# A decode kernel at the memory's pace: three attention pairs with P as the weight, one more unit held on the chip, and new schedule tables

## The chip, the cores and the metric

One core of one Trainium2 chip. The metric is device time in microseconds (us); lower is better. The kernel before was run three times: 304.89 us median, from 302.9 to 305.69.

## The reference

Two layers, each an attention block with a cached K and V and then a gated block, on 4 sequences of one new token each. The weights are the same in both layers, and so are K and V.

```python
B, Sq, D = 4, 1, 512;  Hq, Hkv, Sk, Dh = 32, 8, 4096, 128;  F = 1792
def attn(x):   # x: layer-normed
    q = (x @ wq) -> heads;  k, v repeated 4 times over the heads
    p = softmax(q k^T * Dh**-0.5);  o = p v
    return o @ wo
def glu(x):
    return (sigmoid(x @ w_gate) * (x @ w_up)) @ w_down
for _ in range(2):
    x = x + attn(layernorm(x))
    x = x + glu(layernorm(x))
```

For one sequence b and one K/V head u, K and V have 4096 x 128 bf16 values each, 1 MB. 4 x 8 heads make 32 MB of K and 32 MB of V, and both layers need all of them: 128 MB, if nothing is kept.

## The kernel before, in words

**Units and pairs.** A unit is one head of one sequence in one layer; a pair is two neighbouring heads of a sequence. There are 32 units and 16 pairs in a layer, so 64 units and 32 pairs (`NP`) in all; an entry of `ORDER` is (layer, sequence, pair of heads), and its place in the list is the pair's position. The pairs are worked off in the order of `ORDER`; layer 1 of a sequence may begin as soon as its own layer 0 and its own gated block are done, so layers and sequences are interleaved.

**Slots and held units.** K and V units are loaded whole into 12 slots of 1 MB of on-chip memory. Once the last q of the second layer is computed, the four slices of `wq` become four further slots (`wq_done`). `RET` names for each sequence the heads whose K or V stay in their slot from layer 0 to layer 1 and so are not loaded twice. `LOADS` is the order of all loads, written out by hand as a string: k, v, o (an eighth of `wo`) and s (a part of the three other weights). `pump()` issues loads from SyncE's queue (SP) for as long as a slot is free; each load waits for the last reader of its slot.

**One step.** Step k (the loop over `plan`) works on the scores and the softmax of pair k and, one step later, on PV of pair k-1; `EARLY` marks pairs whose PV is done in their own step. K is turned in place by VectorE's 32x32 transposes (`k_turn`, line 1164), the scores are 16 matmuls a unit (line 1180), the row maximum is a reduction and two small matmuls (1217 to 1253), the exponential runs on ScalarE (1265), P is turned by two matmuls (`ptrans`, 1310) and copied in 16 pieces by ScalarE and VectorE (1338, 1344). PV (`pv`, line 1414) takes **V as the weight**: per unit 32 weight loads of 128x128, and as the moving operand four columns of P, repeated up to the width that `PV_WIDE` gives (32, 48 or 64 columns; the result is in the first four). `normalise` (1505) multiplies by the inverse row sums, `wo_mm` applies `wo` either with `wo` as the weight (1566) or, where `WO_ROW` is set, as rows (1536, a copy at 1545 and a turn of four matmuls at 1549).

**Between the layers.** The gated block of a sequence and its q for layer 1 are 23 small pieces (`pass_steps`: layer norm, gate, up, down, q as rows). `PLACES` says for each piece in which step and at which of nine places (0 to 8) of the step it is issued; `do_steps(k, w)` issues what stands at a place. `FILL` adds matmuls of no use to a place: `fill(n)` multiplies the identity by itself n times (line 1199). `STEP` packs per step where K is turned and PV stands.

**A branch that is not taken.** For `PV_WIDE` below 2, `pv` already has the other form: P as the weight (8 or 16 columns a matmul) and 256 or 512 columns of V moving, into separate strips of 32 rows of a bank; and `o_turn` brings the rows back into columns: ScalarE copies the bank into the slot of the V just read, and 2 or 4 f32 matmuls with a selecting matrix `o_sel` write the columns. No pair of the kernel before uses it, so `o_sel` isn't built.

**The tail.** In step 32 the PV of the last pair (`pv_last`, line 1441) reads V in quarters, the last `wo` product is added up, and the gated block of all four sequences follows (920 to 2053). `LAST`, from the last entry of `STEP`, says whether the `wo` product that is still open goes before or after the first `pv_last`.

Of the kernel before, what the change touches and what calls it, by code (L numbers as in the profile page):

```python
# [5 lines left out]
dt = mybir.dt  # L6
# [13 lines left out]
]  # L20

ORDER = [
    (0, 0, (0,)),
    (0, 0, (3,)),
    (0, 0, (2,)),
    (0, 1, (1,)),
    (0, 0, (1,)),
    (0, 2, (0,)),
# [4 lines left out]
    (0, 1, (2,)),  # L33
    (1, 0, (3,)),
    (1, 0, (0,)),
    (0, 2, (2,)),
    (1, 1, (2,)),
    (1, 1, (3,)),
    (0, 2, (1,)),
    (0, 2, (3,)),  # L40
    (1, 1, (0,)),
    (1, 1, (1,)),
    (0, 3, (3,)),
    (1, 2, (3,)),
    (0, 3, (0,)),
    (0, 3, (2,)),
    (0, 3, (1,)),
    (1, 2, (1,)),
    (1, 2, (0,)),
    (1, 2, (2,)),  # L50
# [12 lines left out]
    ),  # L63
    (
# [10 lines left out]
    ),  # L75
    (
# [16 lines left out]
    "kooookokovkvkkvokokvvvkksvvkksvvksskkssk",  # L93
    "vvvkkvkvkkvvkkvkvkvkvvkvkvkvkvkvkvvkvvkk",
    "kkkvvvvkkvkvkvvkkvvkkvkkvvkvvkkkvvvkvkkv",
    "kvvvkkvkvvkkkvkkvvvvvv",
# [35 lines left out]
WO_ORDER = (1, 3, 7, 2, 4, 0, 6, 5)  # L132

WO_TURN = (
# [7 lines left out]
PV_WIDE = (  # L142
# [4 lines left out]
)  # L147
# [9 lines left out]
WSUM = (  # L157
    (7, 8), (28, 0), (22, 5), (18, 7),
    (22, 0), (29, 7), (27, 4), (29, 7),
# [3 lines left out]
AHEAD = ((29, 2), (30, 8), (32, 4))  # L163
# [147 lines left out]
def bass_interleave_layers__gqa_block_cached__glu_gated_glu__decode_kernel(  # L311
# [85 lines left out]
    norm = sbt([P, KD + 10, Bn], dt.float32, "norm")  # L397
    sq_sb, newt = norm[:, 0:KD + 1, :], norm[:, KD + 1:, :]
    lnsum, blk_f, vpe, nt_a, nt_b, nt_c, nt_y, rs = [newt[:, i, :] for i in range(8)]
    y0i = newt[:, 8, :].bitcast(dt.int32)  # L400
# [259 lines left out]
    def head_masks():  # L660
# [15 lines left out]
        for u in range(2):  # L676
# [30 lines left out]
        id4 = ident_bf.rearrange("p (u e w) -> p u e w", u=2, e=2)  # L707
        dve(
            lambda e: e.tensor_tensor(sel_f[:, :, :], id4[:, :, 0, 0:2], id4[:, :, 1, 0:2], ALU.add),
# [3 lines left out]
        if SEL:  # L713
            dve(
                lambda e: e.tensor_tensor(o_sel[:, :, :], id4[:, :, 0, 0:SEL], id4[:, :, 1, 0:SEL], ALU.add),
                reads=IDENT,
                writes=["o_sel"],
            )
# [754 lines left out]

    def o_turn(g):
        p = g % 2
        many = 2 - PV_WIDE[g]
        s = stage.pop()
        o_raw = slot[s].bitcast(dt.float32)[:, 0:2 * P * many]
        act(lambda e: e.activation(o_raw, O_ps[p][:, 0:2 * P * many], ACTF.Copy), reads=[f"O{p}"], writes=slot_keys(s))
# [16 lines left out]
    def normalise(g):  # L1496
        if PV_WIDE[g] < 2:
            o_turn(g)
# [633 lines left out]
```

## Time and profile before

| | |
|---|---|
| three runs | 302.9, 304.89, 305.69 us |
| profiled execution, span from first to last instruction | 306.1 us (no other time of it is known) |
| mean granted TensorE clock | 0.883 |
| busy | PE 73%, PE's weight loads 51%, VectorE 67%, ScalarE 43%, GpSimd 9% |
| read from memory | 116.66 MB, 381 GB/s over the span |

The profile's first part gives busy time by engine; the second cuts the span in 40 slices of 7.65 us, with the granted TensorE clock, the busy share of the DMA engines and the GB/s of each; the fourth follows the chain of work that ended last back from the end. A matmul's busy time is a model, since matmuls overlap; how long a row of matmuls takes is read from the timeline, where neighbours of one line are merged.

### The profile page before, as it was taken

How to read it: one execution, taken by the hardware profiler on the slowest of the kernel's cores; microseconds unless marked ns; L12 is line 12 of the kernel's file. 1: busy time of each engine (PE TensorE's matmuls, PEld its weight loads, DVE VectorE, ACT ScalarE, POOL GpSimd, SP SyncE). 2: the span in 40 equal slices, each digit the busy share in tenths (PEclk: the TensorE clock that was granted, in tenths of full speed). 3: DMA queues.
4: the chain of work that ended last, by engine and by line, in shares of the span. 5: the costliest groups of instructions: out<-in, count | busy, mean ns of one | idle time of the engine just before them, and what ended most of it. 6: DMA issues, size and time to landing. Idle time of an engine off the chain costs nothing.

```text
span 306.1 us, 11460 instructions
## 1 busy us (share of the span) xinstructions
PE 224.3 (73%) x4993; PEld 157.6 (51%) x4993; DVE 205.7 (67%) x600; ACT 131.2 (43%) x521; POOL 26.0 (9%) x107
## 2 busy tenths in 40 slices
PE   0384386864687888688886777888868688987886
PEld 0331043543464466566554554665546456556676
DVE  4755677885766368875854997566788668357743
ACT  1031243552205246564451874627772443646310
POOL 0000000000000010000001110001000000012200
PEclk9999999999579897979999857589788979599977
DMA  7999999999999979999999999999999999999900
GB/s 283 420 397 415 422 414 416 418 418 421 418 416 403 388 295 418 423 415 416 388 394 378 415 422 421 419 418 422 420 416 418 413 412 415 400 345 411 377 18 3
DMA packets 20094, 117.40 MB, mean 384 GB/s; under 512 B 1992, under 2 KB 1996, under 8 KB 7500
## 3 DMA queue, kind: packets, MB, share of 16 engines
q1 hardware_dynamic: 20044, 116.67, 93.9%
q8 instruction: 39, 0.64, 0.8%
q14 instruction: 11, 0.09, 0.1%
HBM read 116.66 MB, written 0.00 MB: 381 GB/s over the span
## 4 chain that ended last, share of the span: by engine, by line
DMA 45%; PE 30%; DVE 12%; SPq 5%; ACT 4%; issue 3%; POOL 0%; POOLq 0%; DVEq 0%; ACTq 0%
DMA slot<-in_A_v_cache_dram 22%; DMA slot<-in_A_k_cache_dram 12%; PE O_ps L1414 9%; DMA wd<-in_B_w_down_dram 6%; DVE slot L1164 6%; DMA wo<-in_A_wo_dram 5%; PE S_ps L1180 5%; ACT pT L1344 2%; SPq L550 2%; SPq L528 2%; PE M_ps L636 2%; PE O_ps L1566 2%; PE M_ps L1034 1%; PE M_ps L1087 1%; DVE wo L651 1%
## 5 line engine op out<-in xcount | busy, mean ns | idle before, releaser
L1164 DVE STREAM_TRANSPOSE slot<-slot 128x1024 f32<-128x1024 f32 (+1 forms) x61 | 100.9, 1663 | 7.0 <-DMA slot<-in_A_k_cache_dram 6.9
L1344 ACT ACTIVATE pT<-PT 32x64 bf16<-32x64 f32 x392 | 84.3, 215 | 31.9 <-PE PT L1310 26.9
L1414 PE MATMUL O_ps<-pT,slot 128*128 128x32 bf16 (+2 forms) x1888 | 65.8, 190 | 16.2 <-DMA slot<-in_A_v_cache_dram 9.6
L1414 PEld LDWEIGHTS O_ps<-pT,slot 128*128 128x128 bf16 x1888 | 59.6, 101 | 23.3 <-DMA slot<-in_A_v_cache_dram 10.6
L1180 PE MATMUL S_ps<-slot,qz 128*32 128x256 bf16 x1008 | 48.9, 329 | 12.5 <-DVE slot L1164 7.2
L1265 ACT ACTIVATE pe<-S_ps,small 128x256 bf16<-128x256 f32 x32 | 15.2, 474 | 63.3 <-DVE small L1253 63.2
L1180 PEld LDWEIGHTS S_ps<-slot,qz 128*32 128x32 bf16 x1008 | 25.3, 107 | 24.8 <-DVE slot L1164 9.2
L1279 POOL TENSOR_TENSOR small<-small 128x1 f32<-128x1 f32 x64 | 12.4, 193 | 217.6 <-ACT pe L1265 215.1
L646 ACT ACTIVATE wo<-M_ps 128x512 bf16<-128x512 f32 x14 | 8.3, 595 | 35.0 <-PE M_ps L636 35.0
L1338 DVE CAST pT<-PT 32x64 bf16<-32x64 f32 x88 | 19.4, 221 | 5.6 <-PE PT L1310 4.1
L1566 PE MATMUL O_ps<-oT,wo 128*128 128x32 bf16 x576 | 19.7, 188 | 1.1 <-issue 0.5
L636 PE MATMUL M_ps<-wo,row 64*128 64x512 bf16 x56 | 13.3, 565 | 9.1 <-DVE wo L651 5.5
L1566 PEld LDWEIGHTS O_ps<-oT,wo 128*128 128x128 bf16 x576 | 18.2, 101 | 2.1 <-DVE oT L1505 1.1
L1217 DVE TENSOR_REDUCE small<-S_ps 128x1 f32<-128x256 f32 x32 | 13.2, 413 | 8.0 <-PE S_ps L1180 7.8
L903 POOL TENSOR_TENSOR qz<-qc,norm 128x128 bf16<-128x128 bf16 x32 | 12.6, 399 | 45.5 <-ACT qc L889 45.5
L1240 PE MATMUL MS<-row_max,mask_f 128*128 128x16 bf16 x64 | 6.6, 176 | 13.1 <-DVE row_max L1223 12.6
L651 DVE CAST wo<-M_ps 128x512 bf16<-128x512 f32 x14 | 9.5, 680 | 9.6 <-PE M_ps L636 9.5
L1505 DVE TENSOR_TENSOR oT<-O_ps,rden 128x8 bf16<-128x8 f32 x31 | 4.9, 159 | 14.4 <-PE O_ps L1414 9.8
L1240 PEld LDWEIGHTS MS<-row_max,mask_f 128*128 128x128 bf16 x64 | 4.3, 107 | 19.2 <-DVE row_max L1223 17.7
L1199 PE MATMUL MS<-ident_bf 128*128 128x256 bf16 x69 | 12.2, 316 | 0.4
L1310 PE MATMUL PT<-ident_bf,pe 128*128 128x128 bf16 x64 | 10.0, 245 | 2.9 <-ACT pe L1265 2.6
L1253 DVE CUSTOM_DVE_ANT_0 row_max<-MS,small 128x16 bf16<-128x16 f32 x32 | 7.0, 217 | 7.3 <-PE MS L1240 7.1
(143 smaller groups left out, 231.1 us busy)
## 6 DMA issues: line engine op xcount, KB each, us to landing
slot<-in_A_v_cache_dram SPq DMA_DIRECT2D x49, 1024.0 KB, 12.5
slot<-in_A_k_cache_dram SPq DMA_DIRECT2D x43, 1024.0 KB, 11.3
wq<-in_A_wq_dram SPq DMA_DIRECT2D x4, 1024.0 KB, 7.8
wo<-in_A_wo_dram SPq DMA_DIRECT2D x8, 512.0 KB, 15.8
wq<-in_A_v_cache_dram SPq DMA_DIRECT2D x3, 1024.0 KB, 12.3
slot<-in_A_v_cache_dram SPq DMA_DIRECT2D x8, 256.0 KB, 13.6
wg<-in_B_w_gate_dram SPq DMA_DIRECT2D x2, 896.0 KB, 18.9
wu<-in_B_w_up_dram SPq DMA_DIRECT2D x2, 896.0 KB, 16.2
```

The source lines that it names most:

```text
L636: (lambda h, i, rows: lambda e: e.matmul(ps[h][:, :], lhsT=spread_w[i][rows, :], rhs=wo_sb[rows, c + i, :], start=(i == 0), stop=(i == 1), ...
L651: lambda e: e.tensor_copy(wo_sb[:, c + 1, :], ps[1][:, :]),
L903: lambda e: e.tensor_tensor(qz_sb[z][:, :, 0:4 * REP].rearrange("p i (a r) -> p i a r", r=REP), qc_sb[:, b, u:u + 2, :, :].rearrange("p u ...
L1164: dve(lambda e: e.transpose(kf, kf), writes=[f"s{st}"])
L1180: (lambda t, b2, e_, w0, s: lambda e: e.matmul(S_ps[p][32 * s:32 * s + 8 * REP, 0:2 * P], lhsT=qzf[:, w0:w0 + 8 * REP], rhs=ktv[:, :, s, : ...
L1217: lambda e: e.tensor_reduce(m, S_ps[p][:, 0:2 * P], AX.X, ALU.max),
L1265: lambda e: e.activation(to, frm, ACTF.Exp, bias=nm_sb[p], scale=exp_scale, accum_out=sm_sb[p][0],),
L1279: (lambda n: lambda e: e.tensor_tensor(sm_sb[p][n + 1], sm_sb[p][n], top(sm_sb[p][n]), ALU.subtract))(n),
L1338: (lambda dst, frm: lambda e: e.tensor_copy(dst, frm))(dst, frm),
L1344: (lambda dst, frm: lambda e: e.activation(dst, frm, ACTF.Copy))(dst, frm),
L1414: (lambda x, c, j: lambda e: e.matmul(O_ps[p][:, ul * OW:ul * OW + PV_WIDE[g]].rearrange("p (w n) -> p w n", n=REP), lhsT=vv[:, x * JG + c ...
L1566: (lambda c, r: lambda e: e.matmul(wide_out(O_ps[p], OWO + c, nb), lhsT=wo_sb[:, u * REP + r, bass.ds(2 * P * (c // 2) + c % 2, P, step=2) ...
```

## The change

It does five things.

1. `RET`: V of head 4 of sequence 3 is held as well (31 units in place of 30), so one load of 1 MB is gone.
2. `PV_WIDE`: the pairs at positions 1, 27 and 30 take P as the weight (1: 256 columns of V move in each matmul; 0: 512 columns).
3. `divide()` for such a pair is `o_copy` (ScalarE's copy) alone; the matmuls that turn the rows back and `normalise` come at one of four times that `TURN` gives for the step: 0 at once, 1 after `ptrans`, 2 after place 7, 3 in the next step ahead of `sums`.
4. `sel` becomes the first two columns of `o_sel` and two small vectors of the layer norm share a place, which frees the memory for `o_sel`.
5. All tables are chosen anew: the order of the pairs (a few neighbours change places), of the loads, the places of the 23 pieces, which pieces of P VectorE copies (`SHARE`), the fills (122 matmuls in 27 places; before 70 in 16), the form of `wo` by pair, `STEP`, and `LAST` (from 5 to 1: the open `wo` product goes after the first `pv_last`).

```diff
-    {"k": (0, 1, 2, 3, 4, 5), "v": (5,)},
+    {"k": (0, 1, 2, 3, 4, 5), "v": (4, 5)},
...
 PLACES = [
...
-        (1, 8), (2, 1), (2, 1), (2, 1), (2, 1), (2, 1),
-        (2, 2), (2, 2), (2, 2), (2, 3), (2, 4), (2, 6),
-        (2, 8), (3, 1), (3, 2), (3, 3), (3, 3), (3, 5),
-        (3, 5), (3, 5), (3, 5), (3, 6), (3, 6),
+        (1, 8), (2, 1), (2, 1), (2, 1), (2, 1), (2, 1), (2, 1), (2, 1), (2, 2),
+        (2, 4), (2, 4), (2, 6), (2, 6), (3, 0), (3, 0), (3, 0), (3, 0), (3, 0),
+        (3, 0), (3, 1), (3, 3), (3, 6), (3, 6),
...
 WO_ROW = (
...
-    2, 0, 0, 2, 1, 0, 0, 2,
-    0, 0, 0, 2, 0, 0, 1, 0,
-    0, 0, 0, 0, 1, 2, 0, 2,
+    2, 0, 0, 0, 0, 0, 1, 2,
+    0, 0, 2, 0, 0, 0, 0, 0,
+    0, 0, 0, 0, 2, 0, 1, 2,
...
 PV_WIDE = (
-    32, 48, 48, 48, 32, 48, 48, 32,
-    64, 48, 64, 64, 48, 48, 32, 32,
-    32, 48, 64, 32, 32, 64, 64, 48,
-    32, 32, 64, 48, 64, 48, 64, 48,
+    32, 1, 32, 32, 64, 48, 48, 32,
+    32, 64, 64, 64, 64, 48, 64, 48,
+    32, 32, 64, 48, 48, 48, 64, 48,
+    64, 48, 64, 0, 64, 64, 0, 32,
...
 FILL = {
-    (3, 8): 1, (4, 6): 6, (5, 1): 6, (5, 2): 5, (5, 8): 8, (6, 0): 4,
-    (6, 4): 6, (6, 7): 2, (8, 2): 8, (11, 1): 8, (11, 5): 1, (12, 1): 5,
-    (18, 7): 3, (22, 2): 4, (25, 5): 2, (33, 1): 1,
+    (0, 1): 4, (2, 8): 1, (3, 3): 1, (4, 0): 1, (5, 8): 9, (7, 4): 5,
+    (7, 8): 1, (8, 2): 10, (12, 1): 6, (13, 8): 4, (14, 1): 1, (14, 7): 8,
+    (16, 0): 7, (16, 7): 2, (16, 8): 10, (17, 1): 5, (21, 0): 2, (21, 7): 3,
+    (22, 0): 1, (22, 7): 11, (22, 8): 1, (24, 1): 1, (24, 7): 14, (26, 2): 11,
+    (29, 6): 1, (32, 8): 1, (33, 8): 1,
...
+TURN = (
+    3, 0, 2, 3, 0, 2, 3, 2,
+    3, 3, 1, 0, 1, 3, 0, 1,
+    1, 0, 1, 2, 0, 2, 0, 1,
+    0, 0, 3, 0, 1, 1, 2, 3,
+    3,
+)
...
-    sel_f = sbt([P, 2, 2], dt.float32, "sel")
-    SEL = 2 * REP * any(w < 2 for w in PV_WIDE)
-    o_sel = sbt([P, 2, SEL], dt.float32, "o_sel") if SEL else None
+    SEL = 2 * REP * (2 - min(PV_WIDE)) if min(PV_WIDE) < 2 else 0
+    o_sel = sbt([P, 2, max(SEL, 2)], dt.float32, "o_sel")
+    sel_f = o_sel[:, :, 0:2]
...
+    def o_copy(g, k):
+        p = g % 2
+        s = stage.pop()
+        o_raw = slot[s].bitcast(dt.float32)[:, 0:2 * P * (2 - PV_WIDE[g])]
+        act(
+            lambda e: e.activation(o_raw, O_ps[p][:, 0:2 * P * (2 - PV_WIDE[g])], ACTF.Copy),
+            reads=[f"O{p}"],
+            writes=slot_keys(s),
+        )
+        turning.append((g, s, o_raw, k))
+
+    def o_turn():
+        if not turning:
+            return
+        g, s, o_raw, k = turning.pop()
...
-        S.group("pe", fns, reads=slot_keys(s) + ["o_sel"], writes=[f"O{p}"])
+        S.group("pe", fns, reads=slot_keys(s) + ["sel"], writes=[f"O{p}"])
         free.append(s)
         pump()
+        normalise(g)
+        normed[seq[2 * g]] = k
...
         def divide():
+            if PV_WIDE[vg] < 2:
+                o_turn()
+                o_copy(vg, k)
+                if TURN[k] == 0:
+                    o_turn()
+                return
             normalise(vg)
             normed[seq[2 * vg]] = k
...
+        if TURN[k] == 1:
+            o_turn()
         wo_at(3)
         do_steps(k, 7)
         second_turn(2)
+        if TURN[k] == 2 or vg in ends:
+            o_turn()
```

The pieces of sequence 3's pass, the last of the four lists of `PLACES`, are shown since the prediction speaks of them; the step of (2, w) is step 26 and that of (3, w) is step 27 in both kernels.

More of the change, by code (lines that the diff above doesn't have):

```diff
@@ L33 @@
     (0, 1, (2,)),
+    (1, 0, (0,)),
     (1, 0, (3,)),
-    (1, 0, (0,)),
     (0, 2, (2,)),
+    (1, 1, (3,)),
     (1, 1, (2,)),
-    (1, 1, (3,)),
     (0, 2, (1,)),
     (0, 2, (3,)),
+    (1, 1, (1,)),
     (1, 1, (0,)),
-    (1, 1, (1,)),
     (0, 3, (3,)),
     (1, 2, (3,)),
+    (0, 3, (1,)),
     (0, 3, (0,)),
     (0, 3, (2,)),
-    (0, 3, (1,)),
     (1, 2, (1,)),
+    (1, 2, (2,)),
     (1, 2, (0,)),
-    (1, 2, (2,)),
     (1, 3, (2,)),
@@ L129 @@
 )
-WO_ORDER = (1, 3, 7, 2, 4, 0, 6, 5)
+WO_ORDER = (
+    4, 1, 0, 2, 3, 6, 7, 5,
+)
 WO_TURN = (
[4 rows of a table removed]
+    (1, 8), (-1, 0), (1, 5), (0, 7), (-1, 0), (0, 1), (2, 2), (0, 2),
+    (3, 3), (0, 8), (0, 3), (0, 0), (1, 2), (1, 8), (2, 1), (3, 8),
 )
 PV_WIDE = (
[4 rows of a table removed]
[4 rows of a table added]
 )
 FILL = {
[3 rows of a table removed]
-}
[5 rows of a table added]
+}
+TURN = (
[5 rows of a table added]
+)
 WSUM = (
-    (7, 8), (28, 0), (22, 5), (18, 7),
-    (22, 0), (29, 7), (27, 4), (29, 7),
-)
-AHEAD = ((29, 2), (30, 8), (32, 4))
+    (11, 1), (19, 0), (15, 5), (23, 7), (21, 0), (21, 3), (18, 6), (27, 8),
+)
+AHEAD = (
+    (28, 4), (31, 8), (32, 1),
+)
 STEP = (
[5 rows of a table removed]
[5 rows of a table added]
 )
@@ L396, in bass_interleave_layers__gqa_block_cached__glu_gated_glu__decode_kernel @@
     xc_sb = sbt([P, KD, Bn], dt.float32, "xc")
-    norm = sbt([P, KD + 10, Bn], dt.float32, "norm")
+    norm = sbt([P, KD + 9, Bn], dt.float32, "norm")
     sq_sb, newt = norm[:, 0:KD + 1, :], norm[:, KD + 1:, :]
-    lnsum, blk_f, vpe, nt_a, nt_b, nt_c, nt_y, rs = [newt[:, i, :] for i in range(8)]
-    y0i = newt[:, 8, :].bitcast(dt.int32)
+    lnsum, blk_f, vpe, nt_a, nt_b, nt_c, rs = [newt[:, i, :] for i in range(7)]
+    nt_y = nt_b
+    y0i = newt[:, 7, :].bitcast(dt.int32)
     xc_bf = sbt([P, KD, Bn], dt.bfloat16, "xc_bf")
@@ L1472, in bass_interleave_layers__gqa_block_cached__glu_gated_glu__decode_kernel @@
     stage = []
-    def o_turn(g):
+    turning = []
+    def o_copy(g, k):
[6 more added lines that the diff above has]
+            writes=slot_keys(s),
+        )
+        turning.append((g, s, o_raw, k))
[3 more added lines that the diff above has]
+        g, s, o_raw, k = turning.pop()
         p = g % 2
         many = 2 - PV_WIDE[g]
-        s = stage.pop()
-        o_raw = slot[s].bitcast(dt.float32)[:, 0:2 * P * many]
-        act(lambda e: e.activation(o_raw, O_ps[p][:, 0:2 * P * many], ACTF.Copy), reads=[f"O{p}"], writes=slot_keys(s))
         fns = []
@@ L1978, in bass_interleave_layers__gqa_block_cached__glu_gated_glu__decode_kernel @@
                 pump()
-            normalise(sg)
-            normed[seq[2 * sg]] = k
+            if PV_WIDE[sg] < 2:
+                o_turn()
+                o_copy(sg, k)
+                o_turn()
+            else:
+                normalise(sg)
+                normed[seq[2 * sg]] = k
             if sg in ends:
```

26 lines of the change are left out of this document (10 added, 16 removed), and 59 rows, old and new, of tables (EARLY, FIRST_AT, PLACES, SHARE).

## The prediction

> **What bounds the kernel now.** I read the page first: the span, the busy times, the slices and the chain that ended last.
>
> ```profile
> span 306.1 us, 11460 instructions
> PE 224.3 (73%) x4993; PEld 157.6 (51%) x4993; DVE 205.7 (67%) x600; ACT 131.2 (43%) x521; POOL 26.0 (9%) x107
> ...
> DMA  7999999999999979999999999999999999999900
> GB/s 283 420 397 415 422 414 416 418 418 421 418 416 403 388 295 418 423 415 416 388 394 378 415 422 421 419 418 422 420 416 418 413 412 415 400 345 411 377 18 3
> ...
> DMA 45%; PE 30%; DVE 12%; SPq 5%; ACT 4%; issue 3%; POOL 0%; POOLq 0%; DVEq 0%; ACTq 0%
> ```
>
> The DMA engines are busy in nearly every slice, at 415 to 422 GB/s in the undisturbed ones; I use 418. So the kernel is an almost unbroken stream of loads with a tail of two slices without any. To see where that is not the whole truth I cut the span into stages: up to the gap near 108 us, the gap, the long middle, the last pass between the layers, the last pairs, the tail.
>
> ```profile
> 5.00:102.50 97.50, 62.76 (x1083) 37.50 (x1084) 65.42 (x163) 30.75 (x109) 5.21 (x21) 0.93 1.02 415
> 102.50:115.00 12.50, 10.18 (x267) 6.80 (x264) 6.97 (x34) 3.96 (x16) 1.49 (x5) 1.00 0.85 323
> 115.00:242.50 127.50, 100.07 (x2377) 73.58 (x2378) 93.23 (x254) 70.14 (x299) 12.64 (x51) 0.85 1.01 413
> 242.50:259.50 17.00, 12.66 (x310) 9.19 (x310) 13.22 (x30) 7.02 (x27) 1.12 (x5) 0.88 1.00 413
> 259.50:269.70 10.20, 10.13 (x149) 5.98 (x150) 3.56 (x20) 5.30 (x21) 0.39 (x2) 0.53 0.96 386
> 269.70:291.00 21.30, 17.35 (x480) 14.03 (x477) 15.13 (x59) 11.18 (x45) 4.59 (x17) 1.00 1.00 380
> 291.00:306.10 15.10, 11.14 (x349) 10.52 (x345) 5.92 (x35) 1.56 (x6) 0.39 (x2) 0.77 0.03 9
> ...
> 107.50:110.00 2.50, 1.75 (x57) 1.23 (x56) 1.70 (x6) 0.83 (x5) 0.51 (x2) 1.00 0.36 131
> ```
>
> The columns are length, busy time (count) of PE, PEld, DVE, ACT, POOL, then granted clock, DMA share and GB/s. Up to 242.5 us only one hole matters: 131 GB/s for 2.5 us, worth 2.5 x (1 - 131/418) = **1.7 us**. From 259.5 to 269.7 the picture turns over: PE is busy 10.13 of 10.20 us, at a granted clock of 0.53. Is it the bound there? The chain of waits, in order of time, says so:
>
> ```profile
> 239.34 8.69 DMA slot<-in_A_k_cache_dram
> ...
> 248.05 1.85 DVE slot L1164
> ...
> 256.44 0.53 PE M_ps L1016 x8
> ...
> 260.16 0.99 PE O_ps L1566 x32
> ...
> 269.24 0.99 PE O_ps L1414 x32
> ```
>
> The last DMA on the chain lands at 248.05. For the remaining 58 us no DMA is on it, though the DMA engines run at full share until 291. The reader should see two kernels in one: **a stream of loads up to 248 us, then a chain of computation** with the stream running a little ahead of it.
>
> **The held unit.** One load of 1.05 MB less is 1.05 MB / 418 GB/s = 2.5 us of stream. Where? I counted the load strings with `RET` applied. Before, V of head 4 of sequence 3 in layer 1 is the load that ends at 99.25 of 107.25 MB (the 4 MB of `wq` not counted); K of pair 27, the last that a pass waits for, is complete at 93.25 MB, and V of pair 25 at 94.25 MB. After, the two have changed places, at 94.25 and 93.25. So up to the end of the DMA-bound part the same number of bytes is needed, and the saved megabyte lies in the part that computation bounds. It can be worth 2.5 us there, or nothing. PE's idle time between 269.7 and 291 is 21.30 - 17.35 = 3.95 us, some of it behind loads; I take half of the 2.5: **-1.2 us**, ends 0 and -2.5.
>
> **The hole at 108 us.** It opens in step 6, where the gated block waits for `w_down`, and SP waits with the next load for PV of pair 5:
>
> ```profile
> 96.77 6.88 SPq L550 DMA_DIRECT2D slot<-in_A_v_cache_dram  x2
> 108.25 4.16 SPq L550 DMA_DIRECT2D slot<-in_A_k_cache_dram  x4
> ...
> 103.96 0.60 PE L1034 MATMUL M_ps<-wq,xc_bf 128*1 128x512 bf16 x8 [0.46 <-DVE xc_bf L765]
> 104.81 1.71 PE L1034 MATMUL M_ps<-wq,xc_bf 128*1 128x512 bf16 x24
> 107.25 0.96 PE L1414 MATMUL O_ps<-pT,slot 128*128 128x48 bf16 x32
> ```
>
> In the new tables the pieces of this pass still stand ahead of the second PV of step 6; the twelve fills of that step are gone, but they fill waits of PE. The `w_down` load ends at 33.25 MB in both. I take **-0.3 us**, ends -1.7 (the hole gone) and +1.7 (doubled).
>
> **The clock in the last pass.** With the four rows of q above at full clock and the same work at half clock I can price what the clock costs:
>
> ```profile
> 261.48 1.04 PE L1180 MATMUL S_ps<-slot,qz 128*32 128x256 bf16 x16
> 262.63 1.02 PE L1034 MATMUL M_ps<-wq,xc_bf 128*1 128x512 bf16 x8
> 264.16 1.02 PE L1034 MATMUL M_ps<-wq,xc_bf 128*1 128x512 bf16 x8
> 265.12 1.89 PE L1414 MATMUL O_ps<-pT,slot 128*128 128x64 bf16 x32
> 266.94 2.12 PE L1034 MATMUL M_ps<-wq,xc_bf 128*1 128x512 bf16 x16
> 269.10 1.12 PE L1414 MATMUL O_ps<-pT,slot 128*128 128x64 bf16 x32
> ...
> 287.30 0.67 PE L1180 MATMUL S_ps<-wq,qz 128*32 128x256 bf16 x16
> ```
>
> q takes 1.02 + 1.02 + 2.12 = 4.16 us against 0.60 + 1.71 = 2.31; one PV 1.89 against 1.12; a unit of scores 1.04 against 0.67: **3.0 us** in all. The change puts 14 fills at the end of step 24 and 11 into step 26, just before this stage. If they keep the clock up, up to 3.0 us are won. I see no row that ties fills to the clock, and PE is as busy as it can be in the cold stretch; of its three stretches of 3.4 us I give the change one: **-1.0 us**, ends 0 and -3.0.
>
> [...]
>
> **What the fills cost.**
>
> ```profile
> L1199 PE MATMUL MS<-ident_bf 128*128 128x256 bf16 x69 | 12.2, 316 | 0.4
> ...
> 222.50:257.50 35.00, 25.23 (x640) 18.94 (x640) 27.06 (x71) 16.50 (x69) 3.17 (x14) 0.90 1.01 416
> ```
>
> A fill adds 12.2 / 69 = 0.18 us to PE. The new table has 52 more, 9.2 us, of them 33 more in steps 22 to 26 (39 against 6): 5.8 us, into a stretch where PE idles 35.00 - 25.23 = 9.8 us. Up to 248 us they lie beside the stream and cost nothing, as long as they end before the load that PE waits for; without that cover they cost all 5.8. The 11 in step 26 (2.0 us) stand on the computing chain, ahead of the row maximum's matmul; they cover the wait for the gate's tanh and product, of which the chain shows 0.55 us on VectorE (row L1001) and PE idles 17.00 - 12.66 = 4.3 us over that stage. I take **+0.5**, ends 0 and +5.8.
>
> **P as the weight.** The trace has no such matmul. In both forms a unit streams 4096 columns of V: sixteen matmuls of 256, or eight of 512. The nearest rows stream as many: 16 score matmuls of 256 columns in 0.67 us, and 8 rows of q with 512 columns in 0.60 us, both over four strips of the array; the new form uses two strips a unit. So between 0.6 us (as well overlapped) and 1.2 us (half as well), and I take 1.2, against 0.96 to 1.12 for V as the weight: +0.1 to +0.2 us a unit. Then the rows are turned back:
>
> ```profile
> L646 ACT ACTIVATE wo<-M_ps 128x512 bf16<-128x512 f32 x14 | 8.3, 595 | 35.0 <-PE M_ps L636 35.0
> ...
> 281.61 0.61 PE L1536 MATMUL O_ps<-wo,oT 128*2 128x256 bf16 x16
> 282.77 0.64 PE L1549 MATMUL O_ps<-sel,row 128*128 128x4 f32 x4 [0.55 <-ACT row L1545]
> ...
> 292.25 0.31 PE L1566 MATMUL O_ps<-oT,wo 128*128 128x32 bf16 x5
> 293.10 0.99 PE L1566 MATMUL O_ps<-oT,wo 128*128 128x32 bf16 x27 [0.54 <-issue]
> 293.93 1.44 PE L1441 MATMUL O_ps<-slot,slot 128*128 128x48 bf16 x32
> ```
>
> A ScalarE copy of 512 columns is 0.6 us, four f32 matmuls 0.64 us. For pair 1 (256 columns, two matmuls, still in step 2) all of it lies beside the loads: 0. For pair 27 the turn comes after `ptrans` of step 28, and the slot it holds longer delays no load, since by my count of slots every load has been let go by step 28: 0, or 0.6 if PE waits for the copy. For pair 30 the turn opens step 32 and is on the chain: +0.6. Its `wo` product becomes rows, 0.61 + 0.55 (wait) + 0.64 = 1.8 us for 0.31 + 0.99 = 1.3: +0.5. But with `LAST` it now follows the first `pv_last`, which fills a hole of PE: the idle time between 292.25 + 0.31 and 293.10 is 0.5, with the wait ahead of the sums about 0.7. Tail: 0.6 + 0.5 - 0.7 = **+0.4 us**, ends -0.7 and +1.5.
>
> **The sum:** -1.2 - 0.3 - 1.0 + 0.5 + 0.4 = **-1.6 us**. The profiled execution's span is 306.1, so 304.5 there; it lies 1.2 above the median of the three runs, whose 304.89 gives **303.3 us**.
>
> **The rivals.**
>
> *Everything the tables aim at comes true (300.0 us).* The clock holds (-3.0), the stream is 2.5 us shorter and the chain keeps pace (-2.5); fills, tail and hole as in the sum (+0.5 + 0.4 - 0.3): -4.9. For it: both gains need each other, and a faster chain is what lets the shorter stream count. Against it: the chain behind 270 us has PE busy 17.35 of 21.30 us at full clock and gains nothing from the clock.
>
> *The held unit takes the slot that pair 27's K needs (308.2 us, slower).* The unit fills one of 12 slots from step 25 to step 29. By my count of slots, the loads let go by the end of step 25 end at 94.25 MB before, which covers K of pair 27; after, at 93.25, one unit short. Its second half is then let go only in step 26, and needs
>
> ```profile
> slot<-in_A_k_cache_dram SPq DMA_DIRECT2D x43, 1024.0 KB, 11.3
> ```
>
> 11.3 us to land and 1.85 for its turn, against 306.1 / 33 = 9.3 us, a mean step: 3.9 us late, on the chain that ends the kernel. With the tail and hole (+0.1), and clock, fills and shorter stream lost to the wait, +4.0 gives 308.9; the turn's first half can go ahead, -0.7: 308.2. It decides once that load is let go less than 13 us before the scores of pair 27. Against it: a release at the start of step 26 and a thin queue shorten the landing.
>
> *The fills stand ahead of work PE could do (309.5 us, slower).* 5.8 us with no cover in place of 0.5, and the clock term stays: -1.6 + 5.3 = +3.7, 308.6; with the fills of steps 13 to 16 touching the stream as well (5 of 0.18) 309.5. Against it: 9.8 us of idle time there.
>
> **How the numbers follow.** The forecast has 0.43, all gained 0.30, the slot 0.13, the fills 0.14. The forecast's own range is 301.5 to 306: its cases below 301.8 give 0.02 to the gain, and the slower two lose 0.02 to the middle. A difference under 1% (3.0 us) is about what measuring this kernel can't tell from none. So faster by over 1% 0.32, within 0.43, slower 0.25. The range reaches from 298.5 (all gained, and the hole gone too) to 309.5.
>
> **What would show it.** Right: 1.05 MB less read; no DMA on the chain after about 250 us; a granted clock above 0.7 somewhere in the 10 us of the last pass; the hole after `w_down` still there; pair 30's turn 0.6 us on PE at the head of step 32. Wrong: a DMA wait on the chain after 250 us (the slot rival), PE idle under 5 us in the 35 us before the last pass with the scores late (the fills), or the last pass under 8 us and the DMA stream ending 4 us earlier (all gained).

## The result: slower by 1.1%, and the profile after

In 14 runs each the changed kernel took 307.93 us (304.63 to 308.99) and the kernel before 304.27 (301.25 to 306.77). The ratio is **1.0114**, 95% interval 1.0087 to 1.0141. The forecast, 303.3 us, had the wrong sign; the time lies inside its range. Two later sets of runs of the same changed kernel gave 1.0046 and 1.0027, so its loss is a fraction of a per cent to 1.1%; why the sets differ is a question of the experiments. (A ratio leaves out runs that lie more than 1.5% above the fastest of their kernel; a median is over all runs.)

First a trap. The profile of before has a span of 306.1 us, that of the changed kernel 302.6: taken at their word, the two say that the change won 3.5 us. But in two executions that have both, the time is 1.9 to 2.0 us above the span (304.63 and 302.6 here, 304.68 and 302.8 below), so by my estimate the profiled execution of before took about 308.0 us, more than any of its 14 timed runs, and that of the changed kernel was the fastest of its 14. So I took the kernel before once more (`before_again`, 304.68 us) and compare with that. The page of the changed kernel:

```profile
span 302.6 us, 11385 instructions
...
PE 228.3 (75%) x4949; PEld 157.7 (52%) x4949; DVE 207.9 (69%) x612; ACT 129.9 (43%) x511; POOL 26.1 (9%) x107
...
GB/s 281 423 396 412 417 422 413 419 418 421 422 418 395 412 255 417 425 419 422 372 386 402 425 421 416 420 417 415 412 415 423 400 406 388 367 401 412 395 79 3
...
HBM read 115.61 MB, written 0.00 MB: 382 GB/s over the span
...
DMA 37%; PE 37%; DVE 11%; ACT 6%; SPq 5%; issue 3%; POOL 0%; DVEq 0%
```

and of the kernel before, second profile:

```profile
span 302.8 us, 11460 instructions
...
PE 218.7 (72%) x4993; PEld 155.3 (51%) x4993; DVE 205.5 (68%) x600; ACT 131.1 (43%) x521; POOL 26.2 (9%) x107
...
GB/s 283 421 402 410 423 416 413 418 421 416 420 419 396 390 298 422 421 419 418 400 419 405 417 421 419 419 419 419 422 417 420 401 420 420 419 414 405 357 49 3
...
HBM read 116.66 MB, written 0.00 MB: 385 GB/s over the span
```

1.05 MB less is read, as `RET` has it, and yet the mean rate falls by as much, 385 to 382 GB/s: the megabyte doesn't become time. The stages show where; first the changed kernel, then `before_again`, with the columns of the prediction's second table.

```profile
107.50:110.00 2.50, 2.16 (x73) 2.04 (x70) 1.27 (x6) 0.72 (x4) 0.39 (x2) 0.79 0.26 49
115.00:242.50 127.50, 104.99 (x2444) 76.31 (x2441) 94.56 (x257) 70.73 (x299) 12.72 (x51) 0.91 1.01 412
242.50:259.50 17.00, 14.72 (x359) 10.69 (x356) 12.95 (x38) 7.94 (x31) 1.13 (x5) 1.00 1.00 390
259.50:269.70 10.20, 9.15 (x221) 6.48 (x220) 6.86 (x32) 5.93 (x25) 1.15 (x4) 1.00 0.97 386
269.70:291.00 21.30, 18.76 (x408) 13.42 (x407) 14.32 (x58) 10.27 (x40) 4.19 (x17) 1.00 0.93 362
```

```profile
107.50:110.00 2.50, 1.74 (x56) 1.22 (x56) 1.69 (x7) 0.85 (x5) 0.53 (x2) 1.00 0.47 105
115.00:242.50 127.50, 98.05 (x2392) 72.61 (x2392) 93.78 (x255) 70.96 (x302) 12.72 (x51) 0.89 1.01 416
242.50:259.50 17.00, 13.74 (x339) 10.28 (x343) 12.73 (x33) 7.38 (x29) 1.13 (x5) 0.81 1.01 421
259.50:269.70 10.20, 8.93 (x228) 5.89 (x220) 6.65 (x34) 6.97 (x28) 1.15 (x4) 1.00 1.02 419
269.70:291.00 21.30, 16.27 (x425) 13.44 (x426) 13.90 (x55) 9.31 (x37) 4.24 (x17) 0.97 0.88 341
```

Two readings. From 242.5 to 269.7 us the DMA engines show nearly the share of `before_again` (1.00 and 0.97; 1.01 and 1.02 there) but move 390 and 386 GB/s where `before_again` moved 421 and 419. That is 17.0 x 31 + 10.2 x 33 = 0.86 MB less, nearly the whole megabyte saved. And PE is busier in each of these stages, although behind 115 us its granted clock is as high or higher. The last-pass stage, cold in the profile that I predicted from (0.53), is at 1.00 **in this execution of the kernel before too**.

The chain of waits shows what stands there. The changed kernel (`after_again`, also 302.6 us), `before_again`, and a variant from below that holds 30 units in the new tables (`a_hold30`):

```profile
249.35 0.61 PE S_ps L1184 x14
249.98 6.91 DMA slot<-in_A_k_cache_dram
256.91 2.31 DVE slot L1168
```

```profile
237.90 8.67 DMA slot<-in_A_k_cache_dram
246.59 2.12 DVE slot L1164
```

```profile
248.05 10.75 DMA slot<-in_A_k_cache_dram
258.83 2.31 DVE slot L1163
```

Before, the last DMA on the chain lands at 246.6 us. In the new tables a load of K that goes out only when PE has read the scores' slot (249.96) lands at 256.9, and VectorE turns it at once. The prediction named this sign ("a DMA wait on the chain after 250 us") for the rival of the slot. The third fence says that the held unit isn't its cause: with 30 held the wait is there as well, until 258.8. Whether it costs anything is read from the exponentials, ScalarE's timeline, of pairs 27 and 31, in `after_again` and then in `before_again`:

```profile
266.03 0.47 ACT L1269 ACTIVATE pe<-S_ps,small 128x256 bf16<-128x256 f32 x1 [2.13 <-DVE small L1257]
...
287.10 0.47 ACT L1269 ACTIVATE pe<-S_ps,small 128x256 bf16<-128x256 f32 x1 [1.01 <-DVE small L1257]
```

```profile
261.93 0.47 ACT L1265 ACTIVATE pe<-S_ps,small 128x256 bf16<-128x256 f32 x1
...
287.39 0.47 ACT L1265 ACTIVATE pe<-S_ps,small 128x256 bf16<-128x256 f32 x1 [1.50 <-DVE small L1253]
```

Pair 27 is 4.1 us late; pair 31 is 0.3 us early. The wait for K makes little of the 4.1 us, as PE's timeline shows, from pair 27's second scores to the matmuls of its row maximum, again first `after_again`:

```profile
259.85 0.65 PE L1184 MATMUL S_ps<-slot,qz 128*32 128x256 bf16 x16
...
261.63 2.97 PE L1038 MATMUL M_ps<-wq,xc_bf 128*1 128x512 bf16 x24
264.53 1.14 PE L1418 MATMUL O_ps<-pT,slot 128*128 128x64 bf16 x32
265.51 0.20 PE L1244 MATMUL MS<-row_max,mask_f 128*128 128x16 bf16 x2
```

```profile
259.32 0.65 PE L1180 MATMUL S_ps<-slot,qz 128*32 128x256 bf16 x16
...
260.93 0.21 PE L1240 MATMUL MS<-row_max,mask_f 128*128 128x16 bf16 x2
```

The scores are 0.5 us later. The rest is order: in the new tables all 32 matmuls of q and a PV stand on PE ahead of the row maximum, in the old ones only 8 of q do. The delay is paid back within four pairs, in which `before_again` has 3.2 us of the stops of PE described below and `after_again` none, and at the end the two profiles are equal: 302.6 and 302.8 us. So these two executions show what the schedule does, and not the per cent by which the timed runs differ.

### The profile page after: what moved, and what is told of

It reads as the page before. It is cut to its first block, busy times and chain, and to the rows that moved or that the text cites. A ratio compares the mean times of both kernels' runs of the same rounds, so it can differ in the third digit from the quotient of the medians.

```text
span 302.6 us, 11385 instructions
## 1 busy us (share of the span) xinstructions
PE 228.3 (75%) x4949; PEld 157.7 (52%) x4949; DVE 207.9 (69%) x612; ACT 129.9 (43%) x511; POOL 26.1 (9%) x107
## 4 chain that ended last, share of the span: by engine, by line
DMA 37%; PE 37%; DVE 11%; ACT 6%; SPq 5%; issue 3%; POOL 0%; DVEq 0%
DMA slot<-in_A_k_cache_dram 14%; DMA slot<-in_A_v_cache_dram 12%; PE O_ps L1418 9%; DMA wo<-in_A_wo_dram 6%; DMA wd<-in_B_w_down_dram 6%; PE S_ps L1184 5%; DVE slot L1168 5%; PE M_ps L1038 4%; ACT pT L1348 3%; PE O_ps L1583 3%; PE M_ps L645 3%; SPq L537 3%; PE O_ps L1391 2%; SPq L559 2%; ACT pe L1269 1%
## 5 line engine op out<-in xcount | busy, mean ns | idle before, releaser
L1168 DVE STREAM_TRANSPOSE slot<-slot 128x1024 f32<-128x1024 f32 (+1 forms) x60 | 99.2, 1656 | 7.6 <-DMA slot<-in_A_k_cache_dram 7.5
L1348 ACT ACTIVATE pT<-PT 32x64 bf16<-32x64 f32 x380 | 81.8, 215 | 28.7 <-PE PT L1314 23.8
L1418 PE MATMUL O_ps<-pT,slot 128*128 128x64 bf16 (+2 forms) x1728 | 59.8, 190 | 8.5 <-DMA slot<-in_A_v_cache_dram 5.7
L1418 PEld LDWEIGHTS O_ps<-pT,slot 128*128 128x128 bf16 x1728 | 54.5, 100 | 16.4 <-issue 5.9
L1184 PE MATMUL S_ps<-slot,qz 128*32 128x256 bf16 x992 | 46.5, 316 | 13.4 <-DVE slot L1168 10.0
L1184 PEld LDWEIGHTS S_ps<-slot,qz 128*32 128x32 bf16 x992 | 23.9, 104 | 27.0 <-DVE slot L1168 13.8
L1342 DVE CAST pT<-PT 32x64 bf16<-32x64 f32 x100 | 22.1, 221 | 4.2 <-PE PT L1314 2.7
L1203 PE MATMUL MS<-ident_bf 128*128 128x256 bf16 x121 | 18.5, 283 | 1.1 <-DVE rden L1302 0.6
L1203 PEld LDWEIGHTS MS<-ident_bf 128*128 128x128 bf16 x121 | 11.1, 101 | 5.2 <-issue 1.4
L1038 PE MATMUL M_ps<-wq,xc_bf 128*1 128x512 bf16 x128 | 11.5, 435 | 0.9 <-DVE xc_bf L769 0.5
```

The costliest lines, as they stand in the source:

```text
L1038: (lambda k, st: lambda e: e.matmul(M_ps[h][32 * st:32 * st + 1, :], lhsT=xc_bf[:, k, 0:1], rhs=wv[:, k, h, :, st, :], start=(k == 0), sto ...
L1168: dve(lambda e: e.transpose(kf, kf), writes=[f"s{st}"])
L1184: (lambda t, b2, e_, w0, s: lambda e: e.matmul(S_ps[p][32 * s:32 * s + 8 * REP, 0:2 * P], lhsT=qzf[:, w0:w0 + 8 * REP], rhs=ktv[:, :, s, : ...
L1203: lambda e: e.matmul(MS[:, 2 * P:4 * P].rearrange("p (i m) -> p i m", i=2), lhsT=ident_bf[:, :], rhs=wide_id, start=True, stop=True,)
L1342: (lambda dst, frm: lambda e: e.tensor_copy(dst, frm))(dst, frm),
L1348: (lambda dst, frm: lambda e: e.activation(dst, frm, ACTF.Copy))(dst, frm),
```

## The experiments

The theories: **the slot** (the held unit delays K of pair 27), **the turned pairs** (P as the weight costs more than I gave it), **the fills** (they stand ahead of work), and a fourth that came up on the way, **PE's program** (where the pieces in which its instructions are loaded begin and end). Ratios are to the kernel before on the same chip, with 95% intervals.

### The changed kernel again, and each part taken out of it

```diff
 a_hold30:  -    {"k": (0, 1, 2, 3, 4, 5), "v": (4, 5)},
            +    {"k": (0, 1, 2, 3, 4, 5), "v": (5,)},
 a_nofill:  -FILL = { ... 122 matmuls in 27 places ... }
            +FILL = {}
 a_wide:    PV_WIDE at 1, 27, 30:  -1, 0, 0  +48, 48, 64
```

`after_again` is the changed kernel itself.

> The changed kernel once more, as the base of this set and for a second profile. Measured so far: ratio 1.0114 to the kernel before. If the profile of 302.6 us was a lucky one (its time is the lowest of 14 runs), this one's span is 305 to 307 us and the ratio 1.008 to 1.015. If the two profiles are typical, the ratio would be below 1.

> The changed kernel with 30 units held as before: V of head 4 of sequence 3 is loaded a second time, 1 MB more. Theory 'slot' (the held unit takes the slot that pair 27's K needs): 2 to 4 us faster than the changed kernel, ratio 0.998 to 1.005. Theory that the held unit is worth its share of the stream: 1 to 2.5 us slower, 1.015 to 1.020. Theory that it lies beside the chain: no difference, 1.011.

> The changed kernel with all 122 fills left out. Theory 'fills stand ahead of work': 2 to 5 us faster than the changed kernel, ratio 0.995 to 1.005, and a granted clock that hardly falls. Theory 'fills hold the clock': granted clock below 0.85 and 1 to 4 us slower, ratio 1.015 to 1.025. Theory 'tables': within 0.3% of the changed kernel.

> The changed kernel with V as the weight in all pairs again (widths 48, 48 and 64 at positions 1, 27 and 30); all other tables as changed. Theory 'turned pairs': P as the weight costs what its matmuls and the turn take (my working: 0.3 us of PV and 0.64 us of turn a pair, two pairs on the chain), so this runs 1 to 3 us faster than the changed kernel, ratio to before 1.001 to 1.008. Theory 'tables' (the loss is in the schedule chosen anew): no difference, 1.011.

| kernel | ratio | median, us |
|---|---|---|
| `after_again` | 1.0046 (1.0007 to 1.0085) | 305.85 |
| `a_hold30` | 1.0047 (1.0014 to 1.0080) | 305.34 |
| `a_nofill` | 1.0153 (1.0098 to 1.0209) | 309.59 |
| `a_wide` | 1.0228 (1.0176 to 1.0280) | 311.82 |

Within the new tables the held unit isn't seen to be worth anything (1.0047 against 1.0046; by the two intervals 0 us, give or take 1.6), and the kernel without the fills, or without the turned pairs, is slower, by 1.1% and by 1.8%. So none of the three is seen to be what the change loses by. The long middle of `a_nofill`:

```profile
115.00:242.50 127.50, 97.86 (x2335) 72.67 (x2335) 93.74 (x255) 69.67 (x294) 12.63 (x51) 0.81 1.00 405
```

Without fills the granted clock of the long middle is 0.81 in place of 0.91, PE is busy 7 us less, and the stream is slower (405 against 412 GB/s). The runs agree on the clock: over the span a mean of 0.84 without fills (6 runs) and 0.90 in `after_again` (12). So fills went with a higher clock, at the price of PE time, and the kernel with them was the faster one; that the clock alone is the reason isn't shown, since this profile also has stops of PE of 4.1 us in sum, of a kind described below, against 1.4 in `after_again`. Nor did a higher clock go with less time between the two kernels: `before_again` has 0.89 there, a mean clock over its span of 0.84 against the 0.91 of the changed kernel's first profile, and the same time, 304.68 against 304.63 us.

### Each part alone in the old tables

```diff
 b_hold31:  RET[3]["v"] in the kernel before:  -(5,)  +(4, 5)
 b_turn:    the new code with all old tables, and
            PV_WIDE at 1, 27, 30:  -48, 48, 64  +1, 0, 0
 b_hold31_turn:  both
```

> The kernel before, for a second profile. Its times lie between 301 and 307 us and a span is about 1.9 us shorter than the time of its run, so the first profile's span of 306.1 us belongs to a slow run. If so, this span is 300 to 304 us, and the stage from 259.5 to 270 us, where PE was busy throughout at half the clock, is shorter here.

> The kernel before, with V of head 4 of sequence 3 held as well and nothing else changed: 1 MB less to load. Theory 'slot' (what the held unit saves of the stream it takes away again as a slot, between 245 and 270 us): ratio 0.998 to 1.010, and less than 1 MB under way for several of the 5 us marks from 245 to 265 (the kernel before had 1.3 to 2.3 there). Theory 'the stream bounds': 2.5 us faster, 0.990 to 0.994.

> The new code with the tables of the kernel before, and only the pairs at positions 1, 27 and 30 turned to P as the weight (widths 1, 0 and 0; turned back at the times of the new table). Theory 'P as the weight is cheaper on the busy engine' (a_wide lost 1.8% without it): ratio 0.985 to 0.995. Theory 'it only fits the tables chosen with it': 1.000 to 1.010. By my working of before (a turn of 0.64 us on the chain): 1.002.

> The tables of the kernel before with both parts of the change that can be taken alone: 31 units held (alone 0.9975) and the pairs 1, 27 and 30 turned (alone 1.0008). If they add up: 0.995 to 1.001. If the turned pairs' fewer instructions (some 300 less) let the shorter stream count: 0.988 to 0.995. If the moved boundaries decide: anything up to 1.015.

| kernel | ratio | median, us |
|---|---|---|
| `b_hold31` | 0.9975 (0.9932 to 1.0018) | 303.97 |
| `b_turn` | 1.0008 (0.9972 to 1.0043) | 304.10 |
| `b_hold31_turn` | 1.0129 (1.0097 to 1.0160) | 307.73 |

`b_hold31` has the lowest ratio of all kernels tried, and its interval holds 1; no version is shown to beat both kernels. Its profile is the shortest of all, and the last stage shows the megabyte arriving early:

```profile
span 300.5 us, 11458 instructions
```

```profile
269.70:291.00 21.30, 16.93 (x460) 14.15 (x461) 14.14 (x57) 8.95 (x35) 3.93 (x16) 1.00 0.81 311
```

311 GB/s against 341: the stream ends at 287.9 us, worked out from the packets, against 290.5 in `before_again`. In the changed kernel it ends at 290.2, with the same megabyte saved.

The two edits don't add. By their ratios alone, 0.9975 x 1.0008 would be 0.998; together they made 1.013. The stages of one execution each say where the time went; `b_turn`, then `b_hold31_turn` (an execution of 307.8 us; its five runs lie between 307.2 and 307.9):

```profile
102.50:115.00 12.50, 10.18 (x265) 6.84 (x261) 6.98 (x34) 4.01 (x17) 1.50 (x5) 1.00 0.86 330
242.50:259.50 17.00, 14.15 (x347) 10.45 (x347) 13.28 (x32) 7.97 (x32) 1.13 (x5) 0.90 1.00 404
```

```profile
102.50:115.00 12.50, 11.22 (x236) 7.53 (x240) 5.63 (x26) 2.58 (x10) 0.76 (x2) 0.76 0.70 257
242.50:259.50 17.00, 13.44 (x259) 8.40 (x255) 11.39 (x30) 6.84 (x28) 0.74 (x3) 0.60 0.98 377
```

In the pass near 108 us the granted clock was 0.76 in place of 1.00, and the exponential of pair 7 comes at 115.3 us against 113.1. Between those of pairs 25 and 26, with 0.60 against 0.90, another 1.3 us go. That is 3.5 of the 3.7 us between the spans, 306.0 and 302.3 us. Why the clock was lower there, and whether it was so in the other four runs, isn't shown.

### Halves of the tables

In `h_AB` all tables are the new ones up to step and position 15 and the old ones from 16; in `h_BA` the old ones come first, and the new ones, with 31 units held and pairs 27 and 30 turned, follow. At that place both orders have worked off the same pairs and loads. `h_BA30` is `h_BA` with 30 held.

```diff
 h_AB:  +tables[0:16] = new;  tables[16:] = old
 h_BA:  +tables[0:16] = old;  tables[16:] = new
```

> The new tables for steps 0 to 15, the old ones from step 16 on (30 units held, pair 1 turned, V the weight in pairs 27 and 30). Theory 'front' (the loss lies in the first half, with pair 1 and the pass of sequence 0): ratio as the changed kernel, 1.005 to 1.012. Theory 'back': within 0.3% of the kernel before. Theory 'seam' (each set of tables only fits itself): above 1.015.

> The old tables for steps 0 to 15, the new ones from step 16 on (31 units held, pairs 27 and 30 turned). Theory 'front': within 0.3% of the kernel before, or below 1. Theory 'back' (the loss lies behind step 16): 1.005 to 1.012. Theory 'seam': above 1.015, as is h_AB.

> As h_BA (old tables to step 15, new from step 16), but with 30 units held. h_BA was 1.0152, and its stream ran dry from 250 to 255 us. Theory 'slot': 1 to 4 us faster than h_BA, ratio 1.002 to 1.012, no dry stream there. Theory 'tables' (the new places of the last pass cost the time, whatever is held): 1.012 to 1.018.

Measured: 1.0131 (1.0081 to 1.0182), 1.0152 (1.0098 to 1.0206) and 1.0165 (1.0107 to 1.0224). Both hybrids are slower than the old whole, and not faster than the new whole. The loss can't be put into one half, and a cut between the tables costs about as much as the change does, as if they fitted each other. That 31 held units in place of 30 gain nothing is seen again, though `h_BA` and `h_BA30` are from two sets. The profiles show part of it, for one execution each: `h_AB` has a cold last pass as in the profile that I predicted from (granted clock 0.56; 18.0 us from the exponential of pair 26 to that of pair 28, 14.4 in `before_again`), and `h_BA` has two of the stops described next, 2.3 us in sum, near 242 and 248 us.

### PE's program in pieces

The pages list a queue of its own for instructions; here `before_again`, its page and then PE's timeline:

```profile
q8 instruction: 39, 0.64, 0.9%
```

```profile
269.02 0.51 PE L1414 MATMUL O_ps<-pT,slot 128*128 128x48 bf16 x14
270.56 0.62 PE L1414 MATMUL O_ps<-pT,slot 128*128 128x48 bf16 x18 [1.04 <-issue]
...
275.55 0.29 PE L1180 MATMUL S_ps<-slot,qz 128*32 128x256 bf16 x2
276.87 0.40 PE L1180 MATMUL S_ps<-slot,qz 128*32 128x256 bf16 x5 [1.04 <-issue]
```

0.64 MB in 39 transfers are 16 KB each. PE has 2 x 4993 instructions on the page, matmuls and weight loads; if these transfers carry them, 9986 / 39 = 256 go with one, and 9898 / 38 = 260 in the changed kernel. The packets of this queue begin at 268.1 and 274.2 us, and some 1.5 us behind each PE stops in the middle of a row of like matmuls, for 1.04 us, with nothing that the profile shows to wait for. I take it that it waits for its own next instructions; the profile doesn't name them.

These stops differ between kernels and executions: summed over the span behind 50 us, from those of 0.3 us and more, 3.7 us in `before_again`, none in the changed kernel's first profile, 1.4 in `after_again`, 4.1 in `a_nofill`, 13.2 in `a_wide` (the longest of its runs), none in `b_hold31_turn`. So I asked whether the place of the boundaries moves the time. Matmuls of four columns that nobody reads, put into a hole of PE near 25 us, push all later instructions along without touching the schedule; by the count of 256, 64 are half a piece (a matmul stands on the page as two instructions, 4949 on PE and 4949 on PEld), 128 a whole one.

```diff
+    S.group("pe", [lambda e: e.matmul(MS[:, 2 * P:2 * P + 4], lhsT=ident_bf[:, :],
+        rhs=ident_bf[:, 0:4], start=True, stop=True)] * 64, reads=IDENT, writes=["MS", "MSs"])
```

> a_wide (V the weight in all pairs of the changed kernel, 1.0228) with 64 more small matmuls of no use (4 columns each, 128 instructions) at about 25 us, where PE waits for wo: every later boundary of 256 PE instructions moves by half a block. In a_wide's profile PE stood still for 0.7 to 1.9 us at a dozen places with nothing that the profile shows to wait for, each about 1 us after a 16 KB transfer of the instruction queue. Theory 'instruction loading': the stalls move with the boundaries, and the ratio changes by more than 0.7% either way, most likely down to 1.008 to 1.015. Theory 'P as the weight itself is what a_wide lacks': 1.020 to 1.026.

> The changed kernel with the same 64 small matmuls at about 25 us. Its two profiles so far show next to no such stalls behind 50 us. Theory 'instruction loading': with moved boundaries stalls appear, ratio 1.010 to 1.020. Theory that instruction loading plays no part: as the changed kernel, 1.004 to 1.011.

> The changed kernel with 128 small matmuls of no use at about 25 us: with their weight loads 256 instructions, as many as one 16 KB transfer of the instruction queue holds, so the block boundaries of PE's later program lie where the changed kernel has them. Theory 'boundaries' (after_shift's 1.9% came from where the blocks end): back to the changed kernel, ratio within 0.5% of that of after_third in this set, and stalls behind 100 us of under 3 us in sum. Theory 'the extra matmuls themselves cost': as after_shift or more, 1.019 to 1.025.

> The kernel before with the 64 small matmuls of after_shift at about 25 us. Theory 'boundaries': the kernel before has a favourable position of its blocks too, and another costs it time: ratio 1.003 to 1.020. Theory that it is robust (its stream bounds it up to 248 us, its stalls lie in the last 40 us only): 0.998 to 1.004.

> The changed kernel for the third time, on the chip of this set: base for after_shift128, and a third profile. Ratio 1.004 to 1.012 by the two sets so far. If this profile is of one of its runs at 306 us or more, I expect PE stalls of 0.7 us and more behind 16 KB instruction transfers, or a dry stream between 250 and 265 us, that the profiles at 302.6 us do not show.

> The changed kernel with 128 more matmuls of four columns (256 more PE instructions, one whole 16 KB piece of PE's program) in the hole of PE near 25 us, once more, beside the kernel with 192 of them. If it is the place of the boundaries between the pieces that counts, they stand where they stood: ratio to the kernel before 1.002 to 1.008, the changed kernel's own. If the number of added matmuls counts, it is slower than the kernel with 64 (1.0191): 1.02 to 1.04.

> The changed kernel with 192 more matmuls of four columns at the same place (384 more PE instructions, one and a half pieces). Boundaries: they stand half a piece away, as with 64 matmuls, so slower than the kernel with 128: ratio 1.012 to 1.022. Neither place nor number: 1.002 to 1.008, as the changed kernel, and the 1.0191 with 64 was that load's own. Number of matmuls: above the kernel with 128 and above 1.03.

| kernel | no-op matmuls | ratio |
|---|---|---|
| changed, three sets | 0 | 1.0114; 1.0046; 1.0027 (0.9995 to 1.0059, `after_third`) |
| `after_shift` | 64 | 1.0191 (1.0120 to 1.0263) |
| `after_shift128` | 128 | 1.0015 (0.9978 to 1.0052) |
| `after_shift128_b` | 128 | 1.0055 (1.0008 to 1.0103) |
| `after_shift192` | 128 | 0.9983 (0.9946 to 1.0021) |
| `a_wide`, `a_wide_shift` | 0, 64 | 1.0228; 1.0160 (1.0099 to 1.0220) |
| `before_shift` | 64 | 1.0004 (0.9968 to 1.0040) |

**The run that was to decide was not made.** `after_shift192` was meant to put the boundaries half a piece away once more, with 192 matmuls. Its edit has 128, and its trace has 5077 PE matmuls, 4949 + 128, as those of `after_shift128` and `after_shift128_b`: it is the same kernel a third time, and its expectation speaks of a kernel that never ran. So half a piece was tried once on the changed kernel, and gave 1.0191; a whole piece was tried three times, and gave 1.0015, 1.0055 and 0.9983, no slower than no piece. The theory is neither shown nor refuted. Against it speaks that half a piece cost the kernel before nothing (1.0004); `a_wide` moved the other way with it, from 1.0228 to 1.0160, with intervals that overlap.

The traces say this much of the stops themselves. Of the seven profiles of what is in effect the changed schedule, the two with the most stops are the two longest: 8.6 us in sum at a span of 309.9 (`after_shift`), 4.9 at 307.3 (`after_shift128`, where under 3 was expected); the other five have 0 to 1.7 us and spans of 302.6 to 305.1. Each is the longest or nearly the longest execution of its set, so this is what a long execution looks like, and not yet a cause.

And the row says something else. The six sets of this schedule with no piece or a whole one lie between 0.9983 and 1.0114, with a mean of 1.0040 and a standard deviation of 0.0045, more than the half-width of most of their intervals; with `after_shift` the mean of seven is 1.006 and the deviation 0.007. The kernel before in these sets had medians from 303.8 to 305.0 us. So the changed kernel is slower by about half a per cent, which is hardly more than the scatter of the sets, and a part of the 1.1% of the first set belongs to that set. Of the differences above, that of `a_wide` in its own set, 1.8%, stands clear of this scatter, and its second set (with 64 no-ops) gave 1.6%. Those of the hybrids, of `a_nofill` and of `b_hold31_turn`, 1.3 to 1.7%, are at its edge, each from one set.

## Why the prediction was wrong

**The base.** It set the span, 306.1, beside the median of times, 304.89, and found the execution 1.2 us long. With the 1.9 us of `before_again` it was 306.1 + 1.9 = 308.0, 3.1 us long: an unusual one, and one term of the sum came from what was unusual in it.

**The clock in the last pass (-1.0): failed.** The matmuls of q in that stage, before as I read it, `before_again`, the changed kernel, and `after_again`:

```profile
L1034 PE MATMUL M_ps<-wq,xc_bf x32: 584/609/634, 262.6 to 268.4; 128*1 128x512 bf16 x32
```

```profile
L1034 PE MATMUL M_ps<-wq,xc_bf x32: 377/377/378, 260.1 to 263.6; 128*1 128x512 bf16 x32
```

```profile
L1038 PE MATMUL M_ps<-wq,xc_bf x32: 377/378/379, 261.9 to 264.0; 128*1 128x512 bf16 x32
```

```profile
L1038 PE MATMUL M_ps<-wq,xc_bf x32: 377/609/634, 260.6 to 264.0; 128*1 128x512 bf16 x32
```

The columns are least, median and most ns of one. The sign that I had named came, a clock above 0.7. But the kernel before has 377 ns there in its second profile, and the changed kernel 609 in its second. Of the profiles on record, 3 of 7 with the old tables in that stage have a median above 400 ns, and 5 of 13 with the new ones. So the cold stretch comes and goes between executions in both, and the change isn't seen to take it away. What it costs when it comes was priced about right: from pair 26's exponential to pair 28's 17.9 us pass in the profile of before and 14.4 in `before_again`. The step that failed is that one execution's clock was taken for the kernel's, and its end credited to the fills. In the first execution of the kernel before PE was busy 3.40, 3.40 and 3.33 us of the three stretches of 3.4 us from 258.8 to 269.0, each at 0.50; in the second, 8.93 of the stage's 10.20 us at 1.00. That the fills would win one of the three was an estimate, and no run shows it: the stage has 0.83 without the fills (`a_nofill`), and with them 1.00, 0.83 and 0.83 (the changed kernel, `after_again`, `after_third`).

**The held unit (-1.2): not seen in the new tables, not contradicted alone.** Alone it gives -304 x 0.0025 = -0.8 us, from -2.1 to +0.5. In the new tables it gives 0 us, and the 1.6 us either way of that figure still hold the -1.2. What the traces add is that the saved megabyte ends as a slower stream from 242.5 to 269.7 us (390 and 386 GB/s against 421 and 419), which the term had at full rate. Worked out from the issues and the packets of the loads, at 255 us 2.9 MB were under way in `before_again`, and 0.7 and 1.2 MB in the two profiles of the changed kernel, while the engines' share still shows 1.00. That too few loads under way is what slows the stream is argued: `b_hold31` moves only 381 GB/s from 242.5 to 259.5 us with 2.0 MB under way at 255, and its profile is the shortest of all.

**The hole at 108 us (-0.3): within its ends.** 49 GB/s in the first profile after, 105 in `before_again`, 131 in the one I had: 2.2, 1.9 and 1.7 us by the prediction's own formula. In `after_again` it is 246, 1.0 us: the hole, too, differs between executions by as much as the term.

**The fills (+0.5): wrong sign inside the new tables.**

```profile
L1203 PE MATMUL MS<-ident_bf 128*128 128x256 bf16 x121 | 18.5, 283 | 1.1 <-DVE rden L1302 0.6
```

18.5 us of PE, 6.3 more than before, as I had it within 3 us; but without them the kernel is 1.1% slower. I had costed a fill by its time on PE only and counted on the clock in one stage only; in these profiles the clock differs over the 127 us of the middle (0.81 without fills, 0.91 and 0.92 with them).

**P as the weight (+0.4): right alone** (1.0008, that is +0.2 us, from -0.9 to +1.3). The rows of pair 30 in the changed kernel's chain:

```profile
285.52 0.96 PE O_ps L1391 x8
286.62 0.98 PE O_ps L1391 x8
287.63 0.61 ACT slot L1485
288.28 1.06 PE O_ps L1501 x8
```

A unit took 0.97 us where I chose 1.2, between 0.6 and 1.2; the copy 0.61 as priced; the turn 1.06 where I had 0.64: the row that I took it from is two f32 matmuls in the code, which the profile shows as four, and the turn has four, shown as eight. Errors of -0.5 for the pair and +0.4 for the turn cancel.

**The rivals.** That of the slot had the place and the wait right and the cause and the price wrong: K's wait to 256.9 us is there with 30 units held too, it puts the scores of pair 27 off by 0.5 us where 3.9 was priced, and the 4.1 us at its exponential are back by pair 31. Against that of the fills speaks `a_nofill`, which is slower and not faster. Without the terms of the clock and the held unit the sum would have been -0.3 + 0.5 + 0.4 = +0.6 us, 1.002, close to the 1.0027 of the third set; but it still holds the fills' +0.5, whose sign failed as well, so that is luck.

**What stays open:** what makes the new whole slower by that half per cent. `b_hold31_turn` and the hybrids say that parts that cost nothing alone cost over a per cent together. Their profiles, one execution each, show where: in stretches where PE's clock was low and in PE's stops. Both come and go between executions of one kernel, and no run here sets either at will, so neither is shown to be the cause. Nor is it settled why sets of one kernel differ by up to 1.3% (1.0114 and, with a whole piece, 0.9983).

## What to carry to other kernels

Before a stage's wait or clock is priced, see it in a second profile, and set a run's time beside another run's time, not a span beside a time: here a 3 us "cold stretch" came and went between executions of both kernels. Where a megabyte is saved, look at GB/s and not at the DMA share: here it went with a slower stream at the same share (390 against 421 GB/s, at 1.00 and 1.01). When a pair is late, look at PE's order ahead of it before a wait is blamed. Here tables chosen as a whole could not be priced as a sum of their parts; move one part at a time, and repeat the whole in a fresh set before a per cent is believed. And count a variant's matmuls in its trace before its time is read: one of these was not the kernel that its name says.

## What the hardware showed unexpectedly

In `before_again` PE stops in the middle of a row of like matmuls, for 1.04 us and again for 1.04 us, each time some 1.5 us behind the start of a 16 KB transfer of the instruction queue; by its page there is one such transfer per 256 instructions of PE. The stops make from none to 13.2 us in sum over one execution of these kernels (the most in `a_wide`), and the transfers are there without them too: in the changed kernel's first profile they begin at 268.1 and 274.7 us, and PE doesn't stop. The same rows of q took 377 ns a matmul in one execution of a kernel (`before_again`) and 609 in another (`before`). The DMA share didn't tell the rate: from 242.5 to 259.5 us 1.01 stood beside 421 GB/s (`before_again`) and 1.00 beside 390 (the changed kernel). And in the changed kernel's pair 30 eight matmuls of 512 columns with P as the weight took as long as 32 weight loads and matmuls with V as the weight in the profile of before (0.97 against 0.96 to 1.12 us), with 16 instructions in place of 64.
